# Longer margins in the plan of a fused attention, Sinkhorn and expert kernel, and eight fills in front of early products that wait for a transfer

## The chip, the core and the metric

The kernel runs on one core of one Trainium2 chip. The core has five engines with queues of their own: TensorE (PE, its weight loads shown as PEld), VectorE (DVE), ScalarE (ACT), GpSimd (POOL) and SyncE (SP), which here only issues transfers. Each engine takes its instructions strictly in the order in which they stand in its queue. The metric is the time of one execution on the device in microseconds; the median of three runs of the kernel before is 1933.54 us (1932.66 to 1934.42).

## What is computed

First a chunked attention (4 batches, 8 heads, 768 positions, 64 channels), then a layer of 8 experts over its 3072 tokens of 512 channels, with gates that are normalized eight times over rows and columns (Sinkhorn):

```python
for c in range(nc):                       # chunks of 32 queries, window of 56 keys and 8 memories
    scores = scale * np.matmul(q_c, k_full.transpose(0, 1, 3, 2))
    a = np.exp(scores - np.max(scores, axis=-1, keepdims=True))
    out[:, :, c_start:c_end] = np.matmul(a / (a.sum(-1, keepdims=True) + 1e-9), v_full)
...
P = np.exp(logits - logits.max())         # logits = x @ w_gate
for _ in range(8):
    P /= P.sum(1, keepdims=True) + 1e-09
    P /= P.sum(0, keepdims=True) + 1e-09
    P *= N / E
for e in range(E):
    out += P[:, e:e + 1] * (np.maximum(x @ w1[e], 0.0) @ w2[e])
```

## The kernel before

The tokens are cut into six pieces of 512 (u = 0 to 5), and the experts' work into 48 units, one for an expert e and a piece u: 0 to 5 for expert 0, then 5 to 0 for expert 1, and so on in turns. Every matrix is kept as two f16 halves (a rounded value and the rest), so a product is three passes. From the second expert on, and for most of the first, the products are formed by a scheme with seven block products in place of eight.

A unit has two parts. In the hidden part, four column blocks fp = 0 to 3 each run seven groups of matmuls into the PSUM tiles px, py and pz. Between two groups that write the same tile ACT reads it (q1, q6, q5) or DVE does (the tile c), and the next group waits for that. Then ACT and DVE make the two halves of h: ACT a cast of ss into h (L2042), DVE the sums ss (L2006) and the rests (L2050, L2066). In the output part, two token blocks t = 0 and 1 together run seven groups of 24 matmuls into yx, yy and yz. ACT reads them scaled by the gate (y1, y6, y5, L2146), POOL adds what was read to the accumulator acc, which came back from DRAM (L2171), and DVE adds the PSUM tile itself (L2181). The last group writes yx again, and so it waits for DVE's sum over yx, which waits for POOL's addition of y5.

The matmuls of a unit's second pair of blocks and of the next unit's first pair stand between two output parts, so DVE and ACT finish one unit's h while PE is at other products. An expert's weights are prepared beside it: POOL forms sums ws (L668), ACT and DVE split them (L580, L588). Before that DVE takes the greatest magnitude of eight weight tiles of the next expert (mxs, L624), and one PARTITION_ALL_REDUCE on POOL (L536) spreads the result over the partitions.

The order of all this is not written by hand. Each piece of work is a Task with an engine, an assumed cost, a priority and the tasks that it depends on, and Plan.run places the tasks with a clock for every engine: of what can start on an engine it takes the one of least priority value. The order that comes out is what is emitted, engine by engine; nothing is reordered on the chip. A wrong assumption about a duration can therefore put an instruction that is not ready in front of one that PE waits for. OVER is what an engine's clock is set back after a task, the lag is what is added until another engine sees its result, and pad puts fill matmuls (`warm`, L494, on data that nothing reads) into PE's queue where the plan sees PE idle for more than 0.4 us. MOVED shifts the priority of single tasks by their number.

Of the kernel before, what the change touches and what calls it, by code (L numbers as in the profile page):

```python
# [60 lines left out]
APART = 3.6  # L61
FAR = 60.0
COLD = 6.9
OPEN = 1.1
OVER = {"ACT": 0.1, "DVE": 0.08, "POOL": 0.07}


class Task:


    __slots__ = ("eng", "cost", "fn", "prio", "left", "ready", "end", "then", "takes", "frees", "n", "dma", "start", "many")


class Past:
# [52 lines left out]
class Plan:  # L127
# [14 lines left out]
    def add(self, eng, cost, fn, deps=(), prio=0.0, bufs=(), takes=None, frees=None, dma=0.0, many=False):  # L142
        t = Task()
        t.eng, t.cost, t.fn, t.prio, t.takes, t.frees = eng, cost, fn, prio, takes, frees
        t.ready, t.end, t.then, t.n, t.dma = 0.0, None, [], len(self.tasks), dma
        t.many = many
        if dma:
            t.cost = cost * ISSUE
        before = {id(d): d for d in deps if d is not None}
        for b in bufs:  # L150
            assert not b.closed
            before.update({id(d): d for d in b.before})
            b.users.append(t)
        t.left = len(before)
        t.prio += MOVED.get(t.n, 0.0)
        for d in before.values():
            d.then.append(t)
        if frees is not None:
            frees.left += 1
        self.tasks.append(t)  # L160
        return t

    def pad(self, now, at):

        now = max(now, OPEN)
        cold = max(0.0, min(at, COLD) - now)
        for banks in self.free.values():
            if banks and banks[0][0] <= now + 0.2:
                n = int(cold / 0.22) + int((at - now - cold - 0.1) * 0.8 / 0.11)
                if n > 0:  # L170
                    _, bank = heappop(banks)
                    self.fill(bank, n)
                    heappush(banks, (at, bank))
                return
# [28 lines left out]
    def run(self):  # L203
        clock = {e: 0.7 for e in self.ENGINES}
        clock["POOL"] = 1.6
        waiting = {e: [] for e in self.ENGINES}
        able = {e: [] for e in self.ENGINES}
        dma = 0.0
        lanes = ([], [])
        for t in self.tasks:  # L210
            if t.left == 0:
                heappush(waiting[t.eng], (t.ready, t.n, t))
        left = len(self.tasks)
        while left:
            best = None
            for e in self.ENGINES:
                w, a = waiting[e], able[e]
                now = clock[e]
                while w and w[0][0] <= now:
                    _, n, t = heappop(w)  # L220
                    heappush(a, (t.prio, n, t))
                pick = self.next(now, w, a, False)
                if pick is not None and pick[1].many and pick[0] < self.again:
                    other = self.next(now, w, a, True)
                    if other is not None and other[0] <= pick[0] + 0.1:
                        pick = other
                if pick is not None and (best is None or pick[0] < best[0]):
                    best = pick
            assert best is not None, "no task can start"
            at, t, heap = best  # L230
            if t.eng == "PE" and self.fill is not None and at - clock["PE"] > 0.4:
                self.pad(clock["PE"], at)
            heap[:] = [x for x in heap if x[2] is not t]
            heap.sort()
            left -= 1
            bank = None
            if t.takes is not None:
                _, bank = heappop(self.free[t.takes.group])
                t.takes.bank = bank
                t.takes.made = t.takes.make(bank)  # L240
            t.start = at
            if t.dma and at < SETTLED:
                parts = round(t.cost / ISSUE)
                soft = t.eng == "POOL"
                past = lanes[soft]
                when = at
                for _ in range(parts):
                    if len(past) >= 8:
                        when = max(when, past[-8])
                    dma = max(dma, when + (SOFT if soft else LAND)) + t.dma / parts  # L250
                    past.append(dma)
                    when += 0.57 if soft else 0.48
                clock[t.eng] = when
                t.end = dma + SLACK
            elif t.dma and t.eng == "POOL":
                clock["POOL"] = at + 2 * t.cost
                dma = max(dma, at) + t.dma
                t.end = at + 2 * t.cost + 3.2
            elif t.dma:
                at = max(at, dma - BEHIND)  # L260
                t.start = at
                clock[t.eng] = at + t.cost
                dma = max(dma, at + t.cost / 2) + t.dma
                t.end = max(dma, at + t.cost) + 2.6
            else:
                cost = 2.0 * t.cost if t.eng == "PE" and at < COLD else t.cost
                t.end = at + cost
                clock[t.eng] = t.end - OVER.get(t.eng, 0.0)
            if t.many:
                self.again = t.end + APART  # L270
            t.fn()
            if t.frees is not None:
                b = t.frees
                b.left -= 1
                b.end = max(b.end, t.end + 0.15)
                if b.left == 0:
                    heappush(self.free[b.group], (b.end, b.bank))
            lag = 0.0 if t.dma else 0.2 if t.eng == "PE" else 0.07
            for s in t.then:
                s.left -= 1  # L280
                late = lag
                if s.eng == t.eng and not t.dma:
                    late = 0.0
                elif t.dma and self.fill is not None:

                    late = MARGIN if s.prio - t.end > FAR else 0.0
                s.ready = max(s.ready, t.end + late)
                if s.left == 0:
                    heappush(waiting[s.eng], (s.ready, s.n, s))
        self.clock = clock  # L290
# [3 lines left out]
def tile_chunked_attn_sinkhorn_moe(  # L294
# [111 lines left out]
    add = plan.add  # L406
# [52 lines left out]
    def buf(kind, pool, shape, dtype, name, slot=None):  # L459

        return rings[kind].take(
            lambda k: pool.tile(shape, dtype, tag=f"{kind}_{k}", name=name), slot
        )
# [37 lines left out]
    def scales(part, s, u, name, deps, prio, pool=None):  # L501
# [20 lines left out]
        def inverse(a):  # L522
            nc.vector.tensor_scalar_mul(u, a, 2.0**-SHIFT)
            nc.vector.reciprocal(s, u)

        t = add("DVE", 0.16, most, deps, prio)
        if pool is None:

            def everywhere():
                power(a)  # L530
                inverse(a)

            t = add(
                "POOL",
                14.0,
                lambda: nc.gpsimd.partition_all_reduce(a, m, P, bass_isa.ReduceOp.max),  # L536
                [t],
                prio,
            )
            return add("DVE", 0.65, everywhere, [t], prio)  # L540
# [119 lines left out]
    def cut(e, fp, which, st, ld, prio):  # L660
        s = sw[:, e, which - 1 : which] if e > 0 else s1[:, fp : fp + 1]
        ws = buf(
            "ws", comb, [P, 4, 2, P] if which == 1 else [P, 4, DH], F32, f"ws{which}_{e}_{fp}"
        )
        eng = nc.gpsimd

        def tt(i, a, b, op):
            return lambda: eng.tensor_tensor(ws.t[:, i], a(), b(), op=op)  # L668
# [27 lines left out]
            o = wo[e, fp, which][0]  # L696
        sums = []
        for op in ops:
            sums.append(add("POOL", 0.8, tt(*op), [ld] + sums[-1:], prio - 5, [st, ws]))
        deps = [known[e, which], ld]  # L700
        if which == 1:
            parts = [
# [228 lines left out]
    def weights(e, fp, which, prio):  # L931
        st, ld = load(e, fp, which, prio - 25)
        cut(e, fp, which, st, ld, prio)
# [893 lines left out]
    now = [0.0, 1.0]  # L1827
# [27 lines left out]
    def hidden(e, u, fp, hs, use_at, aside, place="h"):  # L1855
# [64 lines left out]
        else:  # L1920
            c = sums_buf("c", [P, 3, GT], f"c_{nm}")
        px, py, pz = psum("px"), psum("py"), psum("pz")
        t1 = run(px, P1, False, [], px)
        q1, r1 = read(px, "q1", t1)
        yield
        t2 = run(py, P2, False, [], py)
        c11 = plus(2, py, q1, [t2, r1])
        yield
        t6 = run(px, P6, True, [r1])
        q6, r6 = read(px, "q6", t6)  # L1930
        yield
# [555 lines left out]
    for fp, s in enumerate(fetch_first(1, START)):  # L2487
# [9 lines left out]
        dma=0.3,  # L2497
# [3 lines left out]
    for n, (e, u) in enumerate(units):  # L2501
# [56 lines left out]
        end = n == len(units) - 1  # L2558
# [23 lines left out]
        if n >= NU and n % NU < NU - 2:  # L2582
# [16 lines left out]
                        dma=7.0,  # L2599
# [36 lines left out]
```

## Time and profile before

| | |
|---|---|
| median of 3 runs | 1933.54 us (1932.66 to 1934.42) |
| the profiled execution | 1932.9 us |
| its span, first to last instruction | 1931.1 us |
| busy share: PE, PEld, DVE, ACT, POOL | 98%, 85%, 74%, 53%, 28% |
| mean granted TensorE clock | 0.995 |
| matmul instructions in the trace | 19609, of them 114 fills |

A busy share is an average over the whole run. PE's busy time counts every matmul up to its modelled end, so PE at 98% tells that it seldom stands still, not that each part of the run is limited by it. Where it does stand still the view of waits names the engine and the line that ended the wait. The mean clock is below 1 because of two stretches that the page's line of the granted clock shows only as two eights among nines.

### The profile page before, as it was taken

The page shows a single profiled execution, that of the slowest core. Times are in us where ns is not written, and L with a number is a line of the kernel's source. Part 1 is how long each engine was busy: PE and PEld are TensorE (multiplying, and loading weights), DVE is VectorE, ACT ScalarE, POOL GpSimd, SP SyncE. Part 2 cuts the span into 40 slices and gives each one's busy share as a digit, 9 for nine tenths or more (in the row PEclk, how much of TensorE's full clock was granted, in tenths as well). Part 3 has the DMA queues.
Part 4 walks back from the last instruction along what each step waited for, and adds up shares of the span by engine and source line. Part 5 has one row for each costly group of instructions (what it writes and reads, how often), then busy time and mean ns, then how long its engine had stood idle before and what let it go on. Part 6 is the DMA issues. An engine that isn't in the chain of part 4 may idle for free.

```text
span 1931.1 us, 47357 instructions
## 1 busy us (share of the span) xinstructions
PE 1895.1 (98%) x19609; PEld 1633.0 (85%) x19609; DVE 1426.3 (74%) x2448; ACT 1020.8 (53%) x2047; POOL 539.3 (28%) x599
## 2 busy tenths in 40 slices
PE   8999999979999999999999999999999999999999
PEld 7777766668888888888888888888888888888888
DVE  5777569867579866888768875897678786786564
ACT  5876665645466445545445544644454454564353
POOL 3341112431134321532124231343114331332112
PEclk9999999989999999999999999999999999999999
DMA  9886654532234432354225433244413632322321
GB/s 206 200 212 177 178 157 148 188 117 94 96 114 158 132 137 83 100 205 160 83 68 185 153 105 126 88 162 152 146 49 125 203 134 88 105 83 83 127 82 66
DMA packets 207127, 254.75 MB, mean 132 GB/s; under 512 B 106112, under 2 KB 140016, under 8 KB 202560
## 3 DMA queue, kind: packets, MB, share of 16 engines
q1 hardware_dynamic: 204960, 249.63, 40.8%
q8 instruction: 153, 2.51, 0.6%
q0 software_dynamic: 1952, 2.11, 0.5%
q14 instruction: 62, 0.51, 0.1%
HBM read 187.83 MB, written 63.44 MB: 130 GB/s over the span
## 4 chain that ended last, share of the span: by engine, by line
PE 81%; DVE 6%; issue 5%; POOL 4%; DMA 2%; ACT 2%; SPq 0%; POOLq 0%; DVEq 0%; ACTq 0%
PE px L1837 21%; PE yx L1837 20%; PE pz L1837 10%; PE yz L1837 9%; PE yp L2434 5%; PE py L1837 5%; PE yy L1837 5%; POOL ws L668 2%; DVE ss L2006 2%; DVE w L588 2%; POOL acc L2171 1%; PE xp L1387 1%; PE sp L1320 1%; DMA acc<-akeep 1%; ACT w L580 1%
## 5 line engine op out<-in xcount | busy, mean ns | idle before, releaser
L1837 PEld LDWEIGHTS <-w 128*128 128x128 f16 x7896 | 771.7, 98 | 99.4 <-issue 8.2
L1837 PEld LDWEIGHTS <-h 128*128 128x128 f16 x7056 | 691.5, 98 | 98.0 <-issue 17.1
L1837 PE MATMUL px<-x,w 128*128 128x256 f16 x4512 | 547.4, 273 | 0.0
L2171 POOL TENSOR_TENSOR acc<-acc,y 128x256 f32<-128x256 f32 x252 | 267.4, 1070 | 946.2 <-ACT y L2146 922.5
L1837 PE MATMUL yx<-w,h 128*128 128x256 f16 x4032 | 469.6, 273 | 16.1 <-DVE acc L2181 16.1
L1897 ACT ACTIVATE q<-px 128x256 f32<-128x256 f32 x376 | 142.3, 383 | 323.6 <-PE px L1837 322.8
L1837 PE MATMUL pz<-x,w 128*128 128x256 f16 x2256 | 278.5, 273 | 7.1 <-ACT q L1897 7.1
L1837 PE MATMUL yz<-w,h 128*128 128x256 f16 x2016 | 233.8, 273 | 0.0
L2066 DVE TENSOR_TENSOR h<-ss,h 128x1024 f16<-128x1024 f32 x168 | 217.8, 1303 | 21.6 <-ACT h L2042 20.5
L2042 ACT CAST h<-ss 128x1024 f16<-128x1024 f32 x168 | 175.4, 1045 | 74.3 <-DVE ss L2006 73.8
L2017 ACT ACTIVATE h<-c 128x768 f16<-128x768 f32 x168 | 138.1, 839 | 104.4 <-DVE c L1907 104.4
L2050 DVE SCALAR_TENSOR_TENSOR h<-c,h 128x768 f16<-128x768 f32 x168 | 165.7, 1004 | 9.0 <-ACT h L2017 9.0
L2006 DVE SCALAR_TENSOR_TENSOR ss<-c,ss 128x256 f32<-128x256 f32 x336 | 168.3, 536 | 0.0
L1907 DVE SCALAR_TENSOR_TENSOR c<-px,q 128x256 f32<-128x256 f32 x188 | 76.0, 421 | 96.6 <-PE px L1837 94.9
L1837 PE MATMUL py<-x,w 128*128 128x256 f16 x1128 | 139.4, 273 | 0.0
L2434 PE MATMUL yp<-w,h 128*128 128x512 f16 x576 | 130.8, 379 | 0.0
L2006 DVE SCALAR_TENSOR_TENSOR ss<-c,h 128x512 f32<-128x512 f32 x168 | 122.9, 750 | 0.0
L2146 ACT ACTIVATE y<-yx,pscale 128x256 f32<-128x256 f32 x168 | 77.8, 470 | 82.1 <-PE yx L1837 81.3
L1907 DVE SCALAR_TENSOR_TENSOR c<-py,q 128x256 f32<-128x256 f32 x188 | 79.1, 421 | 53.8 <-PE py L1837 52.6
L1837 PE MATMUL yy<-w,h 128*128 128x256 f16 x1008 | 116.9, 273 | 0.0
L580 ACT ACTIVATE w<-ws,sw 128x1024 f16<-128x1024 f32 x56 | 64.1, 1145 | 96.8 <-POOL ws L668 96.7
L2434 PEld LDWEIGHTS <-h 128*128 128x128 f16 x576 | 55.5, 98 | 60.4 <-issue 0.6
(194 smaller groups left out, 1773.4 us busy)
## 6 DMA issues: line engine op xcount, KB each, us to landing
x<-xkeep SPq DMA_DIRECT2D x28, 1792.0 KB
akeep<-acc SPq DMA_DIRECT2D x168, 256.0 KB
acc<-akeep SPq DMA_DIRECT2D x168, 256.0 KB
w1f<-in_moe_w_dram SPq DMA_DIRECT2D x36, 512.0 KB
w2f<-in_moe_w_dram SPq DMA_DIRECT2D x32, 512.0 KB
w1fm<-in_moe_w_dram SPq DMA_DIRECT2D x28, 512.0 KB
w2fm<-in_moe_w_dram SPq DMA_DIRECT2D x28, 512.0 KB
xkeep<-x SPq DMA_DIRECT2D x6, 1792.0 KB
```

Of the source, the lines that this page charges most:

```text
L580: lambda: nc.scalar.activation(dst(0), src(), AF.Copy, scale=s),
L1837: nc.tensor.matmul(dst.t, a, b, start=(not more and n == 0), stop=(n == end), skip_group_check=more,)
L1897: lambda: nc.scalar.activation(t.t, src.t, AF.Copy, scale=down),
L1907: lambda: nc.vector.scalar_tensor_tensor(c.t[:, o], src.t, down, q.t, op0=ALU.mult, op1=ALU.add),
L2006: lambda: nc.vector.scalar_tensor_tensor(dst(), src(), 0.0, other(), op0=ALU.max, op1=op),
L2017: lambda: nc.scalar.activation(h.t[:, 0, 0:3], c.t, AF.Relu),
L2042: lambda: nc.scalar.copy(h.t[:, 0, 3:7], ss.t),
L2050: lambda: nc.vector.scalar_tensor_tensor(h.t[:, 1, 0:3].rearrange("p a n -> p (a n)"), c.t.rearrange("p a n -> p (a n)"), 0.0, h.t[:, 0, 0 ...
L2066: lambda: spare.tensor_tensor(h.t[:, 1, 3:7], ss.t, h.t[:, 0, 3:7], op=ALU.subtract),
L2146: (lambda: nc.scalar.activation(t.t, src.t, AF.Copy, scale=f))
L2171: lambda: nc.gpsimd.tensor_tensor(acc.t[:, cols], acc.t[:, cols], q.t, op=ALU.add),
L2434: nc.tensor.matmul(py.t, hf.t[:, hl, where[fh], o : o + P], room(fp, WIDE * wl + DM * fh, WIDE * wl + DM * (fh + 1)), start=(fp == 0 and i ...
```

## The change

Five edits, all in numbers that the plan works with or in how it places fills:

- after plan time 150 an engine's clock is no longer set back after a task (OVER counts as 0);
- for results that are ready after plan time 150 the lag to another engine is 0.12 instead of 0.07 (from PE it stays 0.2);
- POOL's sums for the weights of experts 1 to 7 are assumed to take 0.95 instead of 0.8;
- a task that depends on a transfer is marked wet, and where PE's next task is wet and starts between plan times 8 and 24, at least eight fills go in front of it, whether the plan sees an idle stretch or not;
- outside that stretch fills follow the rule they followed before.

The work itself is the same. The table MOVED is untouched.

```diff
+BRISK = 150.0
+DENSE = 24.0
+MORE = 8
...
-    def pad(self, now, at):
+    def pad(self, now, at, more):
...
-                n = int(cold / 0.22) + int((at - now - cold - 0.1) * 0.8 / 0.11)
+                n = int(cold / 0.22) + max(more, int((at - now - cold - 0.1) * 0.8 / 0.11))
...
-            if t.eng == "PE" and self.fill is not None and at - clock["PE"] > 0.4:
-                self.pad(clock["PE"], at)
+            if t.eng == "PE" and self.fill is not None:
+                more = MORE if t.wet and 8.0 < at < DENSE else 0
+                if more or at - clock["PE"] > 0.4:
+                    self.pad(clock["PE"], at, more)
...
-                clock[t.eng] = t.end - OVER.get(t.eng, 0.0)
+                clock[t.eng] = t.end - (OVER.get(t.eng, 0.0) if at < BRISK else 0.0)
...
-            lag = 0.0 if t.dma else 0.2 if t.eng == "PE" else 0.07
+            lag = 0.0 if t.dma else 0.2 if t.eng == "PE" else 0.07 if t.end < BRISK else 0.12
             for s in t.then:
                 s.left -= 1
+                s.wet |= t.dma > 0
...
-            sums.append(add("POOL", 0.8, tt(*op), [ld] + sums[-1:], prio - 5, [st, ws]))
+            sums.append(add("POOL", 0.8 if e == 0 else 0.95, tt(*op), [ld] + sums[-1:], prio - 5, [st, ws]))
```

What this does to the emitted order: up to the 199th instruction of ACT, the 215th of DVE and the 86th of POOL every queue is as it was, but for 48 fills on PE: eight each in front of the second tx, the first two gram_w, the first gram_v, the first xp and the second tq. Two more fills stand later. From there to the last Sinkhorn product (cp) PE's groups are interleaved in another way. Behind it PE's groups stand exactly as before, and only the other queues differ.

The first place is POOL's queue at the output part of expert 1's first unit (u = 5). The accumulators acc_1_20 to acc_1_23 belong to it; y6 and y5 are what ACT read from yx and yz. Before:

```order
L2171 TENSOR_TENSOR acc_1_22_6350<-acc_1_22_6350,y6_1_5_0_6722 128x256
L2171 TENSOR_TENSOR acc_1_23_6445<-acc_1_23_6445,y6_1_5_1_6737 128x256
L536 ISA
L536 ISA most_of_119<-most_of_119 128x2
L2171 ISA
L2171 TENSOR_TENSOR acc_1_20_6261<-acc_1_20_6261,y5_1_5_0_6759 128x256
L2171 TENSOR_TENSOR acc_1_21_6371<-acc_1_21_6371,y5_1_5_1_6776 128x256
```

And of the change:

```order
L2177 TENSOR_TENSOR acc_1_22_6399<-acc_1_22_6399,y6_1_5_0_6771 128x256
L2177 TENSOR_TENSOR acc_1_23_6513<-acc_1_23_6513,y6_1_5_1_6791 128x256
L2177 TENSOR_TENSOR acc_1_20_6302<-acc_1_20_6302,y5_1_5_0_6807 128x256
L2177 TENSOR_TENSOR acc_1_21_6419<-acc_1_21_6419,y5_1_5_1_6826 128x256
L542 ISA
L542 ISA most_of_119<-most_of_119 128x2
L2177 ISA
```

The all-reduce for expert 2 (the three ISA rows) moved behind the two additions of y5; after it POOL has the next unit's additions.

The second place is ACT's queue in the second unit of an expert (here expert 4, u = 1), where the last blocks of the first unit (h_4_0_2) are still being finished. Before:

```order
L1897 ACTIVATE q6_4_1_0_15577<-px_4_1_0_15515 128x256
L1897 ACTIVATE q6_4_1_1_15587<-px_4_1_1_15524 128x256
L2042 CAST h_4_0_2_15511<-ss_4_0_2_15549 128x1024
L1897 ACTIVATE q5_4_1_0_15609<-pz_4_1_0_15580 128x256
L1897 ACTIVATE q5_4_1_1_15618<-pz_4_1_1_15592 128x256
```

And of the change:

```order
L1903 ACTIVATE q6_4_1_0_15633<-px_4_1_0_15564 128x256
L1903 ACTIVATE q6_4_1_1_15643<-px_4_1_1_15575 128x256
L1903 ACTIVATE q5_4_1_0_15645<-pz_4_1_0_15626 128x256
L1903 ACTIVATE q5_4_1_1_15653<-pz_4_1_1_15635 128x256
L2048 CAST h_4_0_2_15552<-ss_4_0_2_15603 128x1024
```

The cast moved behind both reads q5. Experts 2, 5 and 7 show the same move at the same place.

The third place is DVE's queue in the output part just before that, of the last unit of expert 3, while the first blocks of expert 4 are being finished. Before:

```order
L2066 TENSOR_TENSOR h_4_0_0_15119<-ss_4_0_0_15203,h_4_0_0_15119 128x1024
L624 TENSOR_REDUCE mxs_120<-w2fm_5_0_15009 128x1
L2066 TENSOR_TENSOR h_4_0_1_15144<-ss_4_0_1_15233,h_4_0_1_15144 128x1024
L2181 SCALAR_TENSOR_TENSOR acc_3_0_14944<-yx_3_0_0_15130,pscale_98,acc_3_0_14944 128x256
L2181 SCALAR_TENSOR_TENSOR acc_3_1_14962<-yx_3_0_1_15149,pscale_98,acc_3_1_14962 128x256
L624 TENSOR_REDUCE mxs_120<-w2fm_5_1_15271 128x1
```

And of the change:

```order
L2072 TENSOR_TENSOR h_4_0_0_15177<-ss_4_0_0_15298,h_4_0_0_15177 128x1024
L2187 SCALAR_TENSOR_TENSOR acc_3_0_15004<-yx_3_0_0_15180,pscale_98,acc_3_0_15004 128x256
L2072 TENSOR_TENSOR h_4_0_1_15194<-ss_4_0_1_15321,h_4_0_1_15194 128x1024
L2187 SCALAR_TENSOR_TENSOR acc_3_1_15040<-yx_3_0_1_15198,pscale_98,acc_3_1_15040 128x256
L2187 SCALAR_TENSOR_TENSOR acc_3_2_14929<-yz_3_0_0_15285,pscale_98,acc_3_2_14929 128x256
L630 TENSOR_REDUCE mxs_120<-w1fm_5_0_14988 128x1
```

The sums over yx moved ahead of the second rest of h, and the reduces over expert 5's weights moved behind them; the same is seen at every change of expert from 1 to 5. As the reduces moved, so did the end of the chain that they feed: the DVE step in front of expert 5's all-reduce stood between two sums over yz of unit (4, 0), and now stands behind the second c over py of the hidden blocks that follow.

## Rows read from the trace of the kernel before

**Rows 1.** The page, span and busy time (share) of each engine.
```profile
span 1931.1 us, 47357 instructions
PE 1895.1 (98%) x19609; PEld 1633.0 (85%) x19609; DVE 1426.3 (74%) x2448; ACT 1020.8 (53%) x2047; POOL 539.3 (28%) x599
```

**Rows 2.** The view of waits, PE: total us, times, longest us.
```profile
PE yx L1837 <- DVE acc L2181: 16.1, 6, 11.8
PE pz L1837 <- ACT q L1897: 7.1, 6, 1.3
...
PE cp L1773 <- DVE cs L1745: 1.2, 3, 0.6
```

**Rows 3.** Timeline, PE, 398 to 422: start, us, instruction, count, [idle before, releaser].
```profile
398.51 2.78 PE L1837 MATMUL yx<-w,h 128*128 128x256 f16 x24
401.13 2.78 PE L1837 MATMUL yz<-w,h 128*128 128x256 f16 x24
415.70 4.97 PE L1837 MATMUL yx<-w,h 128*128 128x256 f16 x24 [11.79 <-DVE acc L2181]
420.51 1.47 PE L1837 MATMUL px<-x,w 128*128 128x256 f16 x12
```

**Rows 4.** Timeline, POOL, 395 to 424.
```profile
396.82 3.65 POOL L2171 TENSOR_TENSOR acc<-acc,y 128x256 f32<-128x256 f32 x2 [4.13 <-ACT y L2146]
406.35 0.37 POOL L536 PARTITION_ALL_REDUCE most_of<-most_of  x1 [5.87 <-issue]
414.42 1.40 POOL L2171 TENSOR_TENSOR acc<-acc,y 128x256 f32<-128x256 f32 x2 [7.70 <-ACT w L580]
```

**Rows 5.** Windows: length, busy us (count) by engine, granted clock, DMA.
```profile
14.00:21.00 7.00, 5.95 (x101) 4.86 (x100) 4.83 (x15) 3.08 (x5) 4.10 (x5) 0.51 1.22 258
406.60:420.30 13.70, 4.60 (x23) 3.30 (x23) 4.54 (x11) 5.11 (x8) 1.55 (x4) 0.50 0.25 71
```

**Rows 6.** Timeline, all engines, 1062 to 1068 (second unit of expert 4).
```profile
1062.93 1.48 DVE L2050 SCALAR_TENSOR_TENSOR h<-c,h 128x768 f16<-128x768 f32 x1
1063.56 1.44 POOL L668 TENSOR_TENSOR ws<-w1f,ws 128x256 f32<-128x256 f32 x1
1064.04 1.47 PE L1837 MATMUL px<-x,w 128*128 128x256 f16 x12
...
1065.31 1.04 ACT L2042 CAST h<-ss 128x1024 f16<-128x1024 f32 x1 [2.00 <-DVE ss L2006]
...
1066.69 1.47 PE L1837 MATMUL pz<-x,w 128*128 128x256 f16 x12 [1.18 <-ACT q L1897]
```

**Rows 7.** Timeline, all engines, 1043 to 1048 (last output part of expert 3).
```profile
1043.24 2.78 PE L1837 MATMUL yz<-w,h 128*128 128x256 f16 x24
...
1044.23 1.21 DVE L624 TENSOR_REDUCE mxs<-w2fm 128x1 f32<-128x1024 f32 x1
1045.36 1.21 DVE L2066 TENSOR_TENSOR h<-ss,h 128x1024 f16<-128x1024 f32 x1
...
1047.01 1.25 PE L1837 MATMUL yx<-w,h 128*128 128x256 f16 x10 [0.99 <-DVE acc L2181]
```

**Rows 8.** Timeline, all engines, 344 to 348 (first unit of expert 1).
```profile
345.46 1.15 ACT L580 ACTIVATE w<-ws,sw 128x1024 f16<-128x1024 f32 x1 [2.02 <-POOL ws L668]
...
346.93 0.82 PE L1837 MATMUL pz<-x,w 128*128 128x256 f16 x6 [1.28 <-ACT q L1897]
```

**Rows 9.** Timeline, PE, 10 to 25 (the start).
```profile
11.92 0.63 PE L823 MATMUL gram_w<-w1f 128*128 128x128 bf16 x8 [1.02 <-DMA w1f<-in_moe_w_dram]
...
20.98 0.63 PE L1257 MATMUL tq<-ident,q 128*128 128x128 f32 x4
```

**Rows 10.** Timeline, POOL, 1080 to 1112 (all-reduce for expert 5).
```profile
1089.38 0.37 POOL L536 PARTITION_ALL_REDUCE most_of<-most_of  x1 [6.04 <-DVE acc L2215]
1108.36 2.02 POOL L2171 TENSOR_TENSOR acc<-acc,y 128x256 f32<-128x256 f32 x2 [18.60 <-ACT y L2146]
```

**Rows 11.** The page, groups: busy us, mean ns of one, idle before and releaser.
```profile
L2050 DVE SCALAR_TENSOR_TENSOR h<-c,h 128x768 f16<-128x768 f32 x168 | 165.7, 1004 | 9.0 <-ACT h L2017 9.0
```

More of the change, by code (lines that the diff above doesn't have):

```diff
@@ L68 @@
 class Task:
-    __slots__ = ("eng", "cost", "fn", "prio", "left", "ready", "end", "then", "takes", "frees", "n", "dma", "start", "many")
+    __slots__ = ("eng", "cost", "fn", "prio", "left", "ready", "end", "then", "takes", "frees", "n", "dma", "start", "many", "wet")
 class Past:
@@ L145, in add @@
         t.ready, t.end, t.then, t.n, t.dma = 0.0, None, [], len(self.tasks), dma
-        t.many = many
+        t.many, t.wet = many, False
         if dma:
```

## The prediction

> **What bounds the kernel now.** The page comes first: PE is busy 98% of the span, the next engine 74% [rows 1]. So time can come back where PE stands still or runs at half clock, and hardly anywhere else. The second view is PE's waits. Two kinds stand out behind the attention: yx waits for DVE's sum into acc 6 times, 16.1 us in all, one of them 11.8; pz waits for ACT's read q 6 times, 7.1 us, none over 1.3 [rows 2]. The third is the timeline around these waits. It shows what is queued ahead of the instruction that PE waits for, and it gives what a wait costs: not the idle time but the shift of the next start. In full flow 24 matmuls of 256 columns take 2.62 us from start to start (398.51 to 401.13), 0.109 each, so a group of 12 takes 1.31 [rows 3]. The last view is the windows, for the two stretches at half clock [rows 5].
>
> The order of PE's groups behind the last cp is the same before and after. So each place there can be taken by itself: what does DVE, ACT or POOL now do earlier for the same PE group?
>
> **A, the all-reduce for expert 2.** The yz group at 401.13 would have been followed by yx at 401.13 + 2.62 = 403.75; yx came at 415.70, 11.95 late [rows 3]. The two additions before end on POOL at 396.82 + 3.65 = 400.47. Then come 5.87 idle, the all-reduce with 0.37 and 7.70 idle, 13.95 in all, and only at 414.42 the additions of y5 [rows 4]. The view puts the last 7.70 down to ACT's w; but no w is an input of these additions, and they stand behind the all-reduce in order, so I read all 13.95 as the price of that instruction on POOL's queue. PE starts again at half speed: the granted clock of the stretch is 0.50, its lower level of 1.2 GHz [rows 5], and 24 matmuls take 420.51 − 415.70 = 4.81 where 2.62 is normal, 2.19 lost [rows 3]. In the changed order the additions stand ahead. They can start at 400.47 and take 1.40 [rows 4]; DVE's sum behind them, two with 0.86 as in the row of the third place or less, is through near 402.7, before 403.75. A gives 11.95 + 2.19 = 14.14. What is late next: POOL is blocked from about 401.9 for 13.95, to about 415.8; but PE then has the hidden part of two pairs of blocks, 14 groups of 1.31 = 18.3 us from about 406.4, before the next output part has anything to add. That work covers it. Uncovered it would cost the same 14.
>
> **B, the cast ahead of q5.** In the second unit of expert 4 px starts at 1064.04, and pz should start 1.31 later at 1065.35; it starts at 1066.69, 1.34 late, released by ACT's q. ACT had the cast of h first (1065.31, 1.04 long), and that had waited 2.00 for DVE's ss, which stood behind an operation of 1.48 [rows 6]. The cast now stands behind both reads. Experts 2 to 6 have the same wait: 5 × 1.34 = 6.7. The sixth pz wait is in expert 1's first unit, where ACT's w waited 2.02 for POOL's ws ahead of q [rows 8]; the longer cost of POOL's sums moves this w behind. It lost 1.28 + 0.16 = 1.44; 0.16 is what the start lost beyond the idle time in the other five (1.34 − 1.18). B gives 8.14. The cast itself, and the h that it makes, is needed by an output part a pair of blocks later, over ten groups of 1.31 off; that hides its delay by two reads.
>
> **C, reduces and rests ahead of the sums over yx.** At the end of expert 3 yz starts at 1043.24, so yx should start at 1045.86; it starts at 1047.01, 1.15 late. DVE was at a reduce (1.21) and a rest of h (1.21) before the sum [rows 7]. The sums now stand ahead of them. Four such changes of expert lose 4 × 1.15 = 4.60. The sixth yx wait is 16.1 − 11.8 − 4 × 0.99 = 0.34 [rows 2, 7], with the 0.16 of the restart 0.50. C gives 5.10. What is late next: the reduces feed the next all-reduce, which on POOL moves by about a yz group and two hidden groups, 2.62 + 2 × 1.31 = 5.2. For expert 5 it now starts at 1089.38 and blocks until 1089.38 + 0.37 + 7.70 = 1097.45; POOL's next additions start at 1108.36 [rows 4, 10]. The slack of 10.9 shrinks to 5.7 and is not used up.
>
> **D, the Sinkhorn end.** cp waits 1.2 in all for cs [rows 2]. The longer lag after 150 reorders that stretch; between 0 and 1.2 I take the middle, 0.6.
>
> **E, fills at the start.** 48 fills stand ahead of early products; a batch of 8 takes 8 × 0.109 = 0.87 at full clock. The first gram_w waited 1.02 for its transfer [rows 9], which covers one batch. PE has idle time in 14 to 21 (5.95 busy of 7.00), so several are covered there too. The tq at 20.98 [rows 9], on which the first queries of the attention hang, I take to be late by the uncovered part of its own batch, about 0.6. The bounds: the granted clock in 14 to 21 is 0.51 [rows 5], so if the fills raise it to the full level, the 5.95 busy would take about half, 2.9 less, for a net of −2.3. If it stays at the lower level, a fill costs 0.22, and the 24 of the last three batches cost 24 × 0.22 = 5.3, less some cover: +5. I take +0.6, the row of tq being nearest.
>
> By the Trainium skill ("TensorE: Matmul & The Clock Gate", "What's actually happening") the throttle is the default and activity releases it. The rows agree in so far as the clock is low where PE waits (0.51 and 0.50, [rows 5]); by that rule the start would lie at the −2.3 end and the sum at 1905.7.
>
> **F, new waits.** Longer margins put other instructions behind, and somewhere they will be late. The changed order shows DVE's rests and ACT's casts late at the same five changes of expert. The trace of before doesn't show such a wait; the bounds are 0 and what the kernel pays for the short margins without A, 8.14 + 5.10, less a little: 11.8. The nearest row is the smallest of the six at yx, 0.50: 5 × 0.50 = 2.5.
>
> **The sum.** 1932.9 (the profiled execution; its span is 1931.1) − 14.14 − 8.14 − 5.10 − 0.6 + 0.6 + 2.5 = 1908.0. The median of the runs is 0.6 above the profiled one, so 1908.6.
>
> **Rivals.** *Margins too short.* The plan's gain of 0.05 a step and 0.07 to 0.1 a task is small against what operations vary: the rest at L2050 takes 1.00 in the mean [rows 11], but 1.48 in the row beside POOL's sum [rows 6]. If B and C come back at neighbouring places, A alone is left: 1932.9 − 14.1 + 0.6 = 1919.4. Against it: the order now has the sums and reads ahead of exactly the instructions that were late. 13%.
>
> By the Trainium skill ("SBUF — State Buffer", "SBUF: two separate sides") DVE and GpSimd share a port pair that one instruction locks for its whole length, when DVE's has two inputs in SBUF and GpSimd's reads there. The 1.48 beside a sum of 1.44 on POOL [rows 6] fits that; by this rule stretches come in lengths of whole operations, which such margins do not hold, and the time would be that 1919.4.
>
> *The fills cost.* The clock stays low and the start loses 5: 1908.6 + 4.4 = 1913.0. For it: the wait behind each batch is for a transfer, and fills only fill until it lands. 5%.
>
> *Slower: the all-reduces of experts 3 to 7 land in an output part.* Their reduces moved behind the sums, as the third place shows. If the all-reduce starts over 10.9 later than it did, POOL's additions of y1 wait, up to 14 each, 5 × 14 = 70: 1908.6 + 70 = about 1979. It decides from 10.9; from about 16 (10.9 plus 27.4 / 5) on the kernel is slower than before. The order shows a move of 5.2. 4%.
>
> *A new block before the last cp.* Between plan time 150 and there PE's groups are interleaved anew, and the same kind of blockage as A may come up once: 1908.6 + 14.1 = 1922.7. Against it: there PE waits little now, no more than D's 1.2 in the row shown [rows 2]. 5%.
>
> *The change does not do it.* If the 13.95 on POOL were due to ACT's w, as the view names it, and not to the all-reduce, A stays, and with C in part: about 1932.9 − 8.1 − 5.1 + 3.1 = 1922.8, near the block just told. 2%.
>
> **How the numbers follow.** The forecast has 71%, the rivals 13, 5, 4, 5 and 2. The range: down, all of D (0.6 more), no new wait (2.5) and the start's better end (2.9) give 1908.6 − 6.0 = 1902.6; I take 1902. Up, A alone gives 1919.4, and 0.6 for the median 1920. Only the last three rivals, 11%, lie above, and some of the forecast's own spread below. About what this kernel's timing can tell from no change is 0.2%, 3.9 us. All cases but the slow one lie more than that below 1933.54; for a mixture of several mishaps at once I leave 2%: faster 0.94, same 0.02, slower 0.04.
>
> **What would show it.** In the changed kernel's waits of PE the row of yx behind acc should be near 2 and that of pz behind q near 0. POOL's timeline should have the all-reduce for expert 2 behind the additions of y5, with the same two idle stretches around its 0.37, and no second stretch at half clock. In 14 to 21 the clock tells which end E took; the first tq tells by how much. F is right if what is new is small waits at the five changes of expert. I am wrong if a long wait stands behind another all-reduce, if pz or yx waits come back with other releasers in the same number, or if PE waits between the end of the attention's first half and the last cp.

## The result, and the profile after

| | median of 4 runs | range |
|---|---|---|
| before | 1933.58 us | 1932.66 to 1934.42 |
| changed | 1909.37 us | 1908.78 to 1910.07 |

The ratio is 0.9875 (95% interval 0.9858 to 0.9892). 1908.6 was forecast. Of the executions behind the experiments below, one of e6 and one of e8 ran at a granted clock of 0.556 and 0.904, took 3288 and 2041 us, and are left out of medians and ratios. The two lines of the page that answer to [rows 1]:

```profile
span 1907.4 us, 47491 instructions
PE 1896.2 (99%) x19659; PEld 1636.5 (86%) x19659; DVE 1451.8 (76%) x2448; ACT 1047.4 (55%) x2047; POOL 540.4 (28%) x599
```

PE is busy 1.1 us longer than before, with 50 fills more, in a span that is 23.7 us shorter. So what went was mostly idle time. The view of waits of PE in the changed kernel (total us, times, longest us) answers to [rows 2]:

```profile
PE sp L1326 <- issue: 3.1, 1, 3.1
...
PE px L1843 <- DVE c L1913: 0.9, 2, 0.5
PE yx L1843 <- DVE acc L2187: 0.5, 1, 0.5
```

The waits of pz for q are gone and of the 16.1 at yx 0.5 is left. At the top stands a wait that the kernel before did not have, for nothing that the profile shows. First the place of A, PE and then POOL (start, us, instruction, [idle before, releaser]), which answer to [rows 3, 4]:

```profile
401.01 2.78 PE L1843 MATMUL yz<-w,h 128*128 128x256 f16 x24
403.63 2.78 PE L1843 MATMUL yx<-w,h 128*128 128x256 f16 x24
406.25 1.47 PE L1843 MATMUL px<-x,w 128*128 128x256 f16 x12
```

```profile
399.21 1.31 POOL L2177 TENSOR_TENSOR acc<-acc,y 128x256 f32<-128x256 f32 x1 [0.36 <-ACT y L2152]
407.27 0.38 POOL L542 PARTITION_ALL_REDUCE most_of<-most_of  x1 [6.76 <-DVE acc L2221]
```

yx starts 2.62 behind yz, at full clock, and the all-reduce stands behind the last addition. At the place of B, in the second unit of expert 4 (answers to [rows 6]; ACT's and PE's rows of the timeline of all engines):

```profile
1046.75 1.47 PE L1843 MATMUL px<-x,w 128*128 128x256 f16 x12
1046.95 0.38 ACT L1903 ACTIVATE q<-pz 128x256 f32<-128x256 f32 x1 [0.27 <-PE pz L1843]
...
1048.06 1.47 PE L1843 MATMUL pz<-x,w 128*128 128x256 f16 x12
1048.39 1.05 ACT L2048 CAST h<-ss 128x1024 f16<-128x1024 f32 x1 [1.06 <-DVE ss L2012]
```

pz follows px by 1.31. The cast comes after the reads, and still waits for DVE's ss, with nobody behind it that PE needs. Last the new wait, PE's timeline at the start:

```profile
34.25 0.75 PE L1326 MATMUL sp<-kC,qT 64*32 64x64 f32 x50
38.15 0.33 PE L1326 MATMUL sp<-kC,qT 64*32 64x64 f32 x10 [3.15 <-issue]
...
40.04 2.87 PE L500 MATMUL warm<-pscale 128*128 128x256 bf16 x16
```

PE stops within one group, after 50 of 60 products that read the same tiles, and then runs at half clock for a while: 16 fills take 2.87, where they take 1.91 in the kernel before at full clock.

**Where the time went, by stretches.** Apart from fills both traces hold the same 19495 products, and behind the last cp they come in one order. So the start of the same product can be compared. The table has how much later (+) or earlier (−) than the kernel before a kernel ends a stretch, less what it was late or early at the stretch's begin; the two other kernels are told of below.

| stretch | terms | forecast | changed | margins alone (second run) | fills alone |
|---|---|---|---|---|---|
| start to 103 us | E | +0.6 | +3.8 | 0.0 | +5.2 |
| to the last cp | D | −0.6 | −2.4 | −1.8 | −1.4 |
| behind the last cp | −A −B −C +F | −24.9 | −24.6 | −25.1 | −0.2 |
| sum | | −24.9 | −23.3 | −26.9 | +3.6 |

### The profile page after: what moved, and what is told of

Read it like the earlier page. It is cut to its first block, busy times and chain, and to the rows that moved or that the text cites. A ratio compares the mean times of both kernels' runs of the same rounds, so it can differ in the third digit from the quotient of the medians.

```text
span 1907.4 us, 47491 instructions
## 1 busy us (share of the span) xinstructions
PE 1896.2 (99%) x19659; PEld 1636.5 (86%) x19659; DVE 1451.8 (76%) x2448; ACT 1047.4 (55%) x2047; POOL 540.4 (28%) x599
## 4 chain that ended last, share of the span: by engine, by line
PE 96%; DVE 2%; issue 1%; DMA 0%; ACT 0%; POOL 0%; SPq 0%; DVEq 0%; POOLq 0%; ACTq 0%
PE px L1843 25%; PE yx L1843 22%; PE pz L1843 12%; PE yz L1843 11%; PE yp L2440 7%; PE py L1843 6%; PE yy L1843 6%; PE xp L1393 1%; PE sp L1326 1%; PE warm L500 1%; PE tq L1263 1%; PE tk L1267 1%; PE pp L2355 1%; PE ta L1383 1%; DVE ss L2012 0%
## 5 line engine op out<-in xcount | busy, mean ns | idle before, releaser
L2012 DVE SCALAR_TENSOR_TENSOR ss<-c,ss 128x256 f32<-128x256 f32 x336 | 176.1, 524 | 8.6
```

What stands on the lines that cost most here:

```text
L2012: lambda: nc.vector.scalar_tensor_tensor(dst(), src(), 0.0, other(), op0=ALU.max, op1=op),
```

## The experiments

Theory: the margins bring some 27 us, behind the attention by the three moves A, B and C; the fills cost, since PE comes to an instruction before its code is there. Rivals: the fills pay for themselves by the clock; the wait at sp belongs to that product; the moves are not what took the waits away.

**e1, the margins alone.**

```diff
-MORE = 8
+MORE = 0
```

> The changed kernel without the eight extra fills (MORE = 0; the margins stay). Theory: the fills cost 3.7 us by the end of the attention's first half, 1.4 of them as their own time in front of the second tq and the rest by a wait for PE's code in the sp group; so 1909.4 - 3.7 = 1905.7, with the stretch 14 to 21 at half clock again, no 3.1 us wait at sp, and the short unexplained waits of the kernel before back at PE's instructions 1217 and 1473. Rival: the fills pay for themselves by holding the clock, and the wait at sp comes from somewhere else; then 1909.4 or more, and the wait at sp stays.

1907.32 us (1905.47 to 1907.42), ratio 0.9862 (0.9847 to 0.9877): below the changed kernel's 1909.37, but 1.6 above the 1905.7 expected. No wait at sp but 0.3. The half clock in 14 to 21 did not come back in this execution: see e10. The fills are no gain.

**e2, the fills alone.** The kernel before with the edits at pad and wet; of the margins nothing.

```diff
+                more = MORE if t.wet and 8.0 < at < DENSE else 0
...
+                s.wet |= t.dma > 0
```

> The kernel before with the eight extra fills and none of the margins. Theory: 1933.6 + 3.7 = 1937.3, with the wait of about 3 us at sp in the same place as in the changed kernel, since the order up to there is the same; the waits at yx (16.1) and pz (7.1) as before. Rival: 1933.6 or less.

1935.17 (1933.17 to 1936.54) against 1933.09 on that chip: ratio 1.0009 (0.9999 to 1.0018), 2.1 us slower in the medians, less than the 3.7 expected, and the interval of the ratio still holds no change (e9 and e10 settle it). The profiled execution is one of the long ones. Its waits of PE:

```profile
PE yx L1843 <- DVE acc L2187: 16.4, 6, 12.0
PE pz L1843 <- ACT q L1903: 7.1, 6, 1.3
PE sp L1326 <- issue: 3.9, 1, 3.9
```

All of A, B and C stays, and the wait at sp comes with the fills.

**e3, the same fills with fewer instructions.**

```diff
+        if wide:
+            wp = banks(b).tile([P, 2, 256], F32, tag=f"b{b}", name="warm")
+            two = idle[:, None, 0:256].broadcast_to([P, 2, 256])
+            for _ in range(n // 2):
+                nc.tensor.matmul(wp, idle[:, 0:P], two, start=True, stop=True)
+            return
```

`wide` holds for the batches in front of products that wait for a transfer; two fills of 256 columns become one of 512.

> The changed kernel with each extra batch of fills as four of 512 columns in place of eight of 256: the same time on PE, half the instructions. If the wait at sp is for PE's code, it stands at PE's instruction 1217 whatever that is; with some 50 instructions fewer ahead of it this is in the fills behind tx, the wait ends at about the same moment, and so is about 2 us and not 3.1: the time 1907 to 1908.5. Rival: the wait belongs to the sp group (a transfer or a result that it needs): it stays at sp with 3 us, 1909.4.

1909.18 (1908.12 to 1909.85), 0.9873 (0.9859 to 0.9888): the time was missed, it is hardly below the changed kernel's. The place was met. PE's timeline:

```profile
38.25 0.55 PE L1389 MATMUL ta<-ident,s 128*128 128x128 f32 x3 [0.47 <-ACT s L1371]
39.46 0.27 PE L1389 MATMUL ta<-ident,s 128*128 128x128 f32 x1 [0.67 <-issue]
...
46.05 1.29 PE L2286 MATMUL pp<-x,w 128*128 128x128 f16 x20 [1.30 <-issue]
```

sp runs through; the waits without a releaser are in other groups, again in their midst. Counting PE's instructions in the traces (weight loads, products and the rest) shows what they have in common:

| kernel | PE starts its 1217th at | code transfer | goes on at | wait | 1473rd: wait |
|---|---|---|---|---|---|
| before | 38.37 | 36.43 to 37.46 | 38.84 | 0.47 | 1.04 |
| changed | 34.78 | 35.81 to 36.75 | 38.15 | 3.36 | 0 |
| e2, fills alone | 34.65 | 36.32 to 37.22 | 38.80 | 4.14 | 0 |
| e3, wide fills | 38.52 | 37.10 to 38.04 | 39.46 | 0.94 | 1.52 |
| e1, margins alone | 38.16 | 35.73 to 36.70 | 38.16 | 0 | 0.24 |

(The wait is from start to start, so a little over the idle time.) The unexplained stops are at the 1217th and the 1473rd instruction, 256 apart, whatever product that is. The thirteen traces at full clock have a few more, at the 1729th, 3777th, 5825th and 8641st, all of them multiples of 256 further on, and none at another place. The page has a DMA row for it:

```profile
q8 instruction: 154, 2.52, 0.6%
```

154 transfers of 16 KB; PE has 39448 instructions in this trace, 256 for each transfer. In every trace taken at full clock PE goes on 1.2 to 1.7 us after the end of one, if it was there by then. The transfer itself starts 2.4 to 4.4 us after PE passed the instruction 256 earlier, at a time when data transfers keep the DMA engines full (share 0.93 to 1.07 in 32 to 38). In the kernel before the 256 instructions up to the 1217th hold 21 fills and a wait for ACT, and PE needs 5.8 us for them (32.58 to 38.37). With 48 fills ahead they are the dense groups xp and sp, and PE is through in 1.9 (32.84 to 34.78). That is the wait. That the transfer is what PE waits for is read from these times; no run moved the transfer by itself.

**e4, POOL's cost alone.**

```diff
-            sums.append(add("POOL", 0.8, ...
+            sums.append(add("POOL", 0.8 if e == 0 else 0.95, ...
```

> The kernel before with only POOL's sums for the weights of experts 1 to 7 assumed at 0.95. In its order the all-reduce for expert 2 stands behind y5's additions, the cast stands behind q5 at the second unit of experts 2, 4 and 6 but not of 3 and 5, and DVE's order at the changes of expert is nearly that of before. Theory (each wait goes by itself): 1933.6 - 14.1 - 3 x 1.34 - 1.4 = 1914 with the pz waits at experts 3 and 5 and the yx waits of about 1 left. Rival (A's 14 us needs the longer lag too, since the additions wait for something else): about 1928.

1908.59 (1907.56 to 1910.06), 0.9871 (0.9857 to 0.9886): both expectations were wrong. One number of the margins brings nearly all: behind the last cp its trace is 24.4 ahead. The yx waits are gone, though just ahead of the sum over yx DVE's order at the changes of expert is that of before, a reduce and a rest of h (only the reduce is over another tile). What differs stands some ten microseconds further up. First the kernel before (DVE and POOL, from the timeline of all engines, eight microseconds ahead of [rows 7]):

```profile
1035.27 0.73 POOL L668 TENSOR_TENSOR ws<-w2f 128x256 f32<-128x256 f32 x1
1035.34 0.48 DVE L2181 SCALAR_TENSOR_TENSOR acc<-yy,pscale,acc 128x256 f32<-128x256 f32 x1 [0.62 <-POOL acc L2171]
...
1035.95 1.18 POOL L2171 TENSOR_TENSOR acc<-acc,y 128x256 f32<-128x256 f32 x1
...
1037.16 0.48 DVE L2181 SCALAR_TENSOR_TENSOR acc<-yy,pscale,acc 128x256 f32<-128x256 f32 x1 [0.61 <-POOL acc L2171]
```

A sum ws stands between the two additions of y1; DVE waits 0.62 and 0.61 for POOL, and has no idle time from there to the sum over yx. So everything behind it on DVE is 1.23 late, the sum over yx too, where PE lost 1.15. Then the same of the kernel with POOL's cost alone (below the dots DVE only):

```profile
1013.50 1.32 POOL L674 TENSOR_TENSOR ws<-w2f 128x256 f32<-128x256 f32 x1 [11.10 <-ACT h L2023]
1014.78 2.57 POOL L2177 TENSOR_TENSOR acc<-acc,y 128x256 f32<-128x256 f32 x2
1015.56 1.21 DVE L2012 SCALAR_TENSOR_TENSOR ss<-c,h 128x512 f32<-128x512 f32 x1
1016.69 0.47 DVE L2187 SCALAR_TENSOR_TENSOR acc<-yy,pscale,acc 128x256 f32<-128x256 f32 x1
...
1023.24 1.21 DVE L630 TENSOR_REDUCE mxs<-w1fm 128x1 f32<-128x1024 f32 x1
1024.36 1.21 DVE L2072 TENSOR_TENSOR h<-ss,h 128x1024 f16<-128x1024 f32 x1
1025.50 0.47 DVE L2187 SCALAR_TENSOR_TENSOR acc<-yx,pscale,acc 128x256 f32<-128x256 f32 x1
```

The sum ws stands ahead of both additions, and DVE has a part of ss ahead of the first sum over yy, where it stood idle before. DVE does not wait, and reduce and rest fit ahead of the sum as they stand. Which of the two moves did it, POOL's or DVE's, this run does not separate.

**e5, the all-reduce alone.** Nothing else of the change; PE's order is that of before.

```diff
+HOLD = 395.0
...
+            if name == "wNone_2":
+                t.ready = HOLD
```

wNone_2 is the all-reduce for expert 2.

> The kernel before with one thing moved: the all-reduce for expert 2 may not start before plan time 395, which puts it behind y5's additions; PE's order is that of before, and DVE and ACT differ only in what waits for the all-reduce's result. Theory: A is 14.1 us and stands alone, 1933.1 - 14.1 = 1919.0, with five yx waits of some 4.3 us and six pz waits of 7.1 left. Rival: the block on POOL's queue only moves on and is paid by a later product: 1930 or more.

1918.66 (1917.77 to 1919.78) against 1931.89, 0.9931 (0.9916 to 0.9946); behind the last cp its trace is 14.03 ahead. A stands alone with its 14 us. Its waits of PE, with B and C nearly as they were:

```profile
PE pz L1840 <- ACT q L1900: 7.5, 7, 1.3
PE yx L1840 <- DVE acc L2184: 3.8, 5, 1.0
```

One of these is the place to look at for C, the change from expert 1 to 2. POOL's order there is that of before, with no ws between the additions of y1 (DVE and PE, from the timeline of all engines):

```profile
578.31 0.47 DVE L2184 SCALAR_TENSOR_TENSOR acc<-yy,pscale,acc 128x256 f32<-128x256 f32 x1
...
589.58 2.78 PE L1840 MATMUL yx<-w,h 128*128 128x256 f16 x24 [0.69 <-DVE acc L2184]
```

DVE does not wait for POOL in this stretch, and PE waits for the sum over yx all the same. e2 has 0.68 there, likewise without a wait on DVE.

**e6 and e11, the lag alone** (the same kernel; the rows are e11's).

```diff
-            lag = 0.0 if t.dma else 0.2 if t.eng == "PE" else 0.07
+            lag = 0.0 if t.dma else 0.2 if t.eng == "PE" else 0.07 if t.end < BRISK else 0.12
```

> The kernel before with only the lag of 0.12. In its order the all-reduce for expert 2 stands between the two additions of y5, the cast stands behind q5 at the second unit of experts 2 to 6, POOL's order at the changes of expert is that of before, and DVE's order there is changed for experts 2 and 4 only. Theory: the second half of yx still waits some 10.6 us, B goes in full: 1933.1 - 1.3 - 8.1 = 1923.7, or 1921.4 if the yx waits at experts 2 and 4 go too; those at 3 and 5 stay with 1.0 each. Rival (each place is decided by what POOL does before it, as the run with POOL's cost alone makes likely): the pz waits stay too, and the time is 1930.

> The lag of 0.12 alone again, for its trace. Theory (POOL's order decides, as the 1928.5 of the first run makes likely): a yx wait of some 10.5 us behind the second addition of y5, and waits of pz or px of about 1 at the second unit of experts 2 to 6 although the cast stands behind both reads. Rival (DVE's and ACT's order decides): no such waits there, and the time lost elsewhere.

1928.49 in the median, ratio 0.9984 (0.9975 to 0.9994); e11 1927.36. The first expectation was too hopeful: the cast stands between the two reads q5, not behind both, and DVE's order at the changes of expert is that of before. The trace, PE and ACT:

```profile
402.79 1.47 PE L1843 MATMUL yx<-w,h 128*128 128x256 f16 x12
415.37 2.72 PE L1843 MATMUL yx<-w,h 128*128 128x256 f16 x12 [11.11 <-DVE acc L2187]
```

```profile
1062.20 1.04 ACT L2048 CAST h<-ss 128x1024 f16<-128x1024 f32 x1 [1.35 <-DVE ss L2012]
1062.24 0.82 PE L1843 MATMUL pz<-x,w 128*128 128x256 f16 x6
1063.16 0.38 ACT L1903 ACTIVATE q<-pz 128x256 f32<-128x256 f32 x1
1063.58 0.81 PE L1843 MATMUL pz<-x,w 128*128 128x256 f16 x6 [0.53 <-ACT q L1903]
```

Each culprit moved by one instruction, and the wait moved into the middle of the group that it was ahead of. At A that saves next to nothing (11.11 in place of 11.79); at B half, 0.69 in place of 1.34. At yx the waits stay, at 0.69 to 1.00, and POOL's ws between the additions of y1 too. At the change from expert 1 to 2 this order has such a ws and that of before has none; the wait there is 0.69 for 0.30. But e2 and e5 have 0.68 and 0.69 without that ws, so this rise shows nothing about POOL.

**e7, OVER alone.**

```diff
-                clock[t.eng] = t.end - OVER.get(t.eng, 0.0)
+                clock[t.eng] = t.end - (OVER.get(t.eng, 0.0) if at < BRISK else 0.0)
```

> The kernel before with only OVER counted as 0 after plan time 150. In its order the all-reduce stands behind y5's additions, the cast stands behind q5 everywhere, POOL's order at the changes of expert is that of before (a sum ws between the two additions of y1), and DVE's is partly that of before at experts 2, 4 and 6. Theory (DVE's order decides): A, B and the yx waits at 3 and 5 go: 1933.1 - 14.1 - 8.1 - 2.3 = 1908.6, yx waits of about 1 at 2 and 4 stay. Rival (POOL's order decides): yx waits of 1 stay at 3 and 5 as well: 1911.

1912.33 (1909.84 to 1912.78), 0.9895 (0.9881 to 0.991). No wait of pz or yx is in its view; POOL's order is that of before at experts 2 to 5, and DVE's has the sum over yx ahead of the second rest of h. So C can be had on DVE alone, and the yx waits that both expectations left did not stay. In exchange px waits, and the time is above both expectations:

```profile
PE px L1843 <- DVE c L1913: 3.1, 6, 0.7
...
PE px L1843 <- ACT q L1903: 1.9, 4, 1.1
```

Behind the last cp it is 19.8 ahead, 5 less than the margins together.

**e8, fewer instructions in all fills, without the extra ones.** The fill of e3 for every fill, and:

```diff
-MORE = 8
+MORE = 0
```

> The changed kernel without the eight extra fills, and every other pair of fills as one product of 512 columns: the same time on PE, some 50 products fewer. If PE's unexplained waits are for its code, they stand at its instructions 1217 and 1473 again, and as PE comes there later they are under 0.3 us together: 1905.5 to 1907. Rival: the waits belong to the products at which they stood (pp), and stay there with up to 2 us: 1907.3 as in the run with the margins only.

1906.87 against 1931.89, 0.9871 (0.9851 to 0.989). There is no wait at the 1217th or 1473rd instruction (0.00 and 0.01); PE gets to the 1217th at 39.43, 1.73 behind the end of its transfer. But PE waits for transfers and for ACT there instead, and the time cannot be told from that of e1. The place shows the cause here, the time does not.

**e9 and e10, the changed kernel and the margins alone, side by side.**

> The changed kernel as it is, beside the next run on the same chip. Theory (the fills cost about 2 us, most of it a wait for PE's code that differs from run to run): 1.5 to 2.5 above the margins alone, and in its trace an unexplained wait of PE at its instruction 1217 again, ending some 1.4 us after the end of a transfer of its code. Rival (the 2 us were the chips and not the fills): within 0.7 of it.

> The margins alone again (MORE = 0), on the same chip as the run before. Theory: 1.5 to 2.5 below the changed kernel. Rival: within 0.7.

1908.65 (1907.41 to 1910.79) and 1906.48 (1906.02 to 1906.86) on one chip; the ratios to before are 0.9878 (0.9863 to 0.9892) and 0.9865 (0.985 to 0.988). The two ranges are apart: the fills cost 2.2 us. The changed kernel stopped again at its 1217th instruction, 2.62, till 1.21 behind the transfer's end. The windows from 14 to 21 us of the changed kernel, of e10 and of e1 (columns as in [rows 5]):

```profile
14.00:21.00 7.00, 6.65 (x127) 5.35 (x126) 4.42 (x14) 3.08 (x5) 5.34 (x7) 1.00 1.13 248
```

```profile
14.00:21.00 7.00, 5.49 (x97) 4.50 (x97) 4.33 (x13) 2.46 (x4) 4.21 (x5) 0.54 1.17 248
```

```profile
14.00:21.00 7.00, 4.69 (x107) 3.66 (x104) 5.26 (x18) 3.08 (x5) 4.39 (x5) 1.00 1.22 258
```

The clock was 1.00 there in all four traces that have the fills; of the nine at full clock else without them, e1 has 1.00 and the others 0.51 to 0.76. But e10 at half clock was as quick as e1 (at 103 us the two are 0.2 apart): there PE waits for transfers, at either level.

**e12, POOL's sums at 1.05,** margins without fills.

```diff
-            sums.append(add("POOL", 0.8 if e == 0 else 0.95, ...
+            sums.append(add("POOL", 0.8 if e == 0 else 1.05, ...
```

> The margins without the extra fills, and POOL's sums assumed at 1.05 in place of 0.95. Behind the last cp the margins alone lose some 3 us in small waits, at most that can come back. Theory (what the plan assumes of POOL decides): 0.5 to 2 below the margins alone. Rival: sums pushed further back delay the weights or the additions: 1 to 5 above.

1906.68 (1905.73 to 1907.82), 0.9868 (0.9852 to 0.9885): the same as e10 within what this can tell, so neither expectation came. Its yx waits are 2.0 in 5 times, those of e10 0.5 in one. No version was clearly below the margins without the fills, which are below both kernels.

## Why the prediction was right

**A was right as worked out**, in size and in cause: 14.14 forecast; 14.14 in the changed kernel's trace (from yz over yx to px the shift goes from −0.12 to −14.26), and the same in e5's (1.02 to −13.12), where nothing else was moved. The releaser that the view named, ACT's w, was not it: e5 left w behind the all-reduce, as it was.

**B was right in size**: all six waits are gone, and the starts behind them gain 8.4 for 8.14 forecast. The cause given, the cast ahead of q5, is shown by e11, where half a move took half of the wait. It is not the only one: in e4 the cast of expert 3 still stands ahead of q5 and only 0.34 is left, since DVE's ss comes earlier.

**C was a little too large and incomplete in cause.** Four changes of expert gave 0.95 to 1.16 each, 4.4 together; the fifth, from expert 1 to 2, for which 0.50 was counted, still waits 0.47 at yx. The step said that the sum over yx was late because a reduce and a rest of h stand ahead of it. They stand there in e4 too, without a wait. At the change that the forecast read, DVE had also waited 1.23 for POOL, ten microseconds before; either was enough for PE's 1.15. The forecast looked at the instructions just ahead of the late one, and not at the idle time further up the same queue. Nor is that idle time the whole cause: at the change from expert 1 to 2 in e5 and e2 there is none, and PE waits 0.69 and 0.68. What counts is when DVE is through with all that is queued up to the sum. In the changed kernel both are moved.

**F was right in size**: 27.4 less 24.6 leaves 2.8, for 2.5 forecast; counted step by step, the shifts that go the wrong way add up to 2.4. They are not evenly at five changes of expert: 0.96 at that from 1 to 2 (at yx, and at px behind c), 0.79 at that from 3 to 4.

**D was too small by its own rule.** It took the idle time of cp, 1.2, as the most that there was to gain. Elsewhere the forecast counted the shift of the next start. Counted so the three cp came 2.0 late before, 0.5 in the changed kernel, and the stretch as a whole brought 1.3 and 1.8 in the two traces with the margins alone. But 1.2 of the changed kernel's 2.4 is not the Sinkhorn end. It is a stop at PE's 5825th instruction that the trace of before has:

```profile
163.50 0.42 PE L1387 MATMUL xp<-v_pair,at 64*32 64x65 f32 x20 [0.98 <-issue]
```

The changed kernel, both traces of the margins alone and e2 do not stop there, and each gains 1.2 at that product; for e2, with the order of before, that is nearly all of its 1.4. The stop is not bound to the old order: of the traces with it, e5 and e11 stop there too, e4 does not. So this half of D is chance, and the cp alone brought about what the forecast had set as the most.

**E was the worst term**: +0.6 forecast, 3.8 in the changed kernel's trace and 2.2 in the medians of e9 and e10. The tq that was to show it came at 22.36 for 20.98, 1.4 late in place of 0.6. The larger part was not in the sum at all: what instructions cost by being instructions, ahead of a place where their transfer is late. The row for it was in the view of waits before (two short waits of pp with no releaser, 1.1 in all, and one of xp, 1.0), and I passed over it. The upper bound of +5 covered it, for another reason than the one given. By the Trainium skill ("TensorE: Matmul & The Clock Gate", "What's actually happening") activity releases the throttle. With the fills the trace agrees: the clock is 1.00 in 14 to 21, for 0.51 before. The gain of 2.3 that the forecast set beside it did not come, since PE was not what this stretch waited for. (The page's line of the granted clock before shows one of the two stretches at half clock, as a single eight; this one is seen in the windows alone.)

The errors of E (+3.2) and D (−1.8) go against each other, and of D's 1.2 is chance. That the sum was met within 0.8 is half luck; that the gain is 24 to 25 us is not.

**The rivals.** Margins too short (1919.4) did not come: both waits went, and the rests of h took 1.01 in the mean, as before [rows 11]. No all-reduce reached an output part: for expert 5 it stands at 1073.48, and POOL's next addition comes 15.6 later. No block came ahead of the last cp.

## What to carry to other kernels

When an instruction is late, go up its engine's queue to the last idle time, ask who ended that, and count all that is queued since; what stands just ahead of it may only be in line. In a plan for queues that run in order an assumed cost that is a little too small can matter much: POOL's sums took 0.87 us in the mean (0.72 to 2.12) and were planned at 0.8; 0.15 us more was worth nearly as much as all margins, and another 0.10 brought nothing. Instructions that fill idle time are not free where code comes in by transfers and dense small products follow: 48 of them cost 2.2 us here.

## What the runs showed of the hardware

- PE's code comes in transfers of 16 KB, 256 instructions each. With the DMA engines full, the one told of here started 2.4 to 4.4 us after PE passed the instruction 256 earlier and took 0.9 to 1.0, and PE went on 1.2 to 1.7 after its end. The profile shows the wait as "issue", in every trace that has one at the 1217th instruction or a multiple of 256 behind it.
- An all-reduce over the partitions shows 0.37 us on POOL and keeps its queue for 14: 5.87, 0.37 and 7.70 in the kernel before, 6.67, 0.37 and 7.49 in e11, with an addition ready behind it each time; moved behind the additions it gave 14.14 back.
